# Long convolution's filter in two shifted copies instead of four, loaded early on two queues, and zero products on the score banks

## The chip, the cores and the metric

The kernel runs on one core of a Trainium2 chip. The core has a matrix engine (PE, with its weight loads shown apart as PEld), a vector engine (DVE), a scalar engine that computes activations (ACT), a general engine (POOL), a queue engine that mostly issues DMA transfers (SP), and 16 DMA engines. Each engine works through its own instructions in order and waits on semaphores. The matrix engine writes to PSUM, of eight banks of 128 x 512 float values. The metric is the device time of one execution in microseconds (us), taken over several runs; the profile is one further execution, with its own time.

## What is computed

Two independent parts, whose results stand side by side in the output (2048 x 1024, bf16):

```python
# A: attention over x (2048 x 512), 32 heads of 16
qkv = x @ wqkv
p = softmax(q @ k.T * 16 ** -0.5)          # 32 heads, 2048 x 2048 scores each
a = (p @ v) @ wo
# B: gated long convolution over q, k, v (2048 x 512 each)
k_shift = causal convolution of k with 4 taps (shift_k), per channel
kv = k_shift * v
y  = causal convolution of kv with ssm_k (2048 taps, per channel) + kv * ssm_D
b  = q * y
```

## The kernel before

The program is written out in full by a planner in Python: it walks through *steps* T = 0, 1, 2, ... and keeps a model of the time of each engine (`pe.t`, `act.t`, `dve.t`) to decide which instruction goes into which engine's stream next. On the chip each engine then simply runs its stream in that order. Nothing is decided at run time, so a transfer that lands later than the model thinks makes the engine that needs it wait, and everything behind that instruction in its stream with it. A DMA's landing is modelled as a fixed time after its issue (4 us, `dma`, line 281), and an issue on SP as 0.05 us.

**Attention.** The 2048 score blocks (128 keys x 512 queries of one head, one PSUM bank each) are taken two or three to a step. In step T, PE computes the scores into banks 0 to 2 or 3 to 5 by turns (line 719), ACT takes the exponential of all of them in one instruction (line 726), and two steps later PE multiplies with V into bank 6 or 7 (line 835). One block of some steps is not given to ACT: DVE computes its exponential by bit arithmetic (line 744, then six passes, lines 784 to 791, in sets of two, later four blocks). `dve_choice` (line 646) decides where; before the filter copies are all made (`h_kzall`) it lets DVE be at most 1.0 us behind, after that 8.0 us, and sets of two start at least 4 steps apart until step 90.

**Background work.** In the first half PE also computes the projections K, V and Q from x, in bank 5 until step 55 and bank 7 later; DVE evacuates each such bank (lines 444, 462, 430). PE's next job needs the bank free, and PE works in order: if the evacuation is late, the next scores are late too. From step 128 on PE does the convolution (line 992): for each group of 4 channels and each of 16 lags, four products of 64 columns. When PE would have little to do, `keep_share` (line 1146) adds products of an identity matrix with zeros (line 1160) to a bank where an accumulation is open (bank 6 or 7), since the chip lowers PE's clock when PE idles; `filler_home` says which bank, or none.

**The filter's way.** For the convolution, the 2048 taps of each channel must be there reversed and shifted, as a matrix that PE can read as its moving operand. The taps come in two loads `KZN[0]` and `KZN[1]` (1 MB each; in the profile they appear under the names of the tiles they lie in, QT and EI), and D in one of 1 KB (`DSS`, in the profile JNK); all three raise one semaphore, `h_kzl`. `kz_first` adds D to the first tap on POOL (tile KZ0, in the profile KZ). For each of 4 channel groups c and each of VG = 4 shifts ro, that is for 16 copies i, `kz_turn` writes a reversed copy in runs of VG values into slot i % 4 of `KZS` (tile WR in the profile): two large DVE copies (`half` 0 and 1, line 512) and a small one (line 518). `kz_store` then stores it to DRAM (`kz_scratch`), on SP; a slot is written again only when its store has landed (`h_kzs.get(i - 4)` in the waits). The pieces are due at steps `KZ_AT + 3 * i + j` (line 539), so copy i = 0 at step 11, copy 4 at step 23 and copy 15 at 56. During the convolution the filter is read back in pieces of 256 KB (line 968) as rows of 1024 values, of which each product takes 64 columns as 64 / VG runs of VG values (line 991).

**The queue SP.** Its first transfers, in this order: x rows 0 to 511; four turned (transposing) loads of x rows 512 to 1023 (`load_x(1)`); the rest of the Q and K weights; four turned loads `load_x(2)`; KZN[0], KZN[1], DSS; four turned loads `load_x(3)`; the first 128 channels of k turned (2048 rows); the first half of v; the next 128 channels of k turned. All stores of filter copies come behind these. ACT issues the first Q and K weights, all V weights and the taps `SHK`, and then begins to compute.

## Time and profile before

| | us |
|---|---|
| median of 3 runs (lowest to highest) | 832.82 (829.57 to 833.69) |
| the profiled execution, its own time | 830.77 |
| its span, from first to last instruction | 828.9 |
| granted clock of PE, mean over the span | 0.994 |

How to read it: rows of groups give line, engine, operation, output tile <- input tiles, shape and count, then busy time and the mean duration of one in ns, then the engine's idle time just before them and who ended it. Rows in order of time begin with start and duration in us; in square brackets stands the idle time before and what ended it. In the windows, the granted clock is 1.00 at full speed. Busy times of PE are modelled and overlap.

### The profile page before, as it was taken

To read this page: it belongs to the slowest core of one execution; us is meant where nothing else is said; L and a number is where in the kernel's file an instruction comes from. 1 tells how busy PE (TensorE), PEld (TensorE's weight loads), DVE (VectorE), ACT (ScalarE), POOL (GpSimd) and SP (SyncE) were. 2 spreads that over 40 slices of the span, in tenths; PEclk is the share of its full clock that TensorE was granted. 3 is DMA by queue.
4 is the path that set the end of the run, shared out by engine and by line. 5 is a ranking of instruction groups with operands and counts; after the bars stand their busy time and mean duration, and the time that the engine had idled before them with its cause. 6 is when DMAs were issued, how large, how long until landed. Compare 5 with 4: busy or idle time off the path is not lost.

```text
span 828.9 us, 29863 instructions
## 1 busy us (share of the span) xinstructions
PE 719.2 (87%) x13409; PEld 320.7 (39%) x13445; DVE 787.6 (95%) x1228; ACT 810.6 (98%) x702; POOL 17.3 (2%) x35
## 2 busy tenths in 40 slices
...
GB/s 244 288 253 269 178 1 48 30 98 282 235 95 195 219 184 216 138 259 296 233 210 274 234 260 263 231 254 238 226 264 307 274 286 299 229 225 187 26 1 26
DMA packets 123855, 167.30 MB, mean 202 GB/s; under 512 B 50384, under 2 KB 55504, under 8 KB 123472
## 3 DMA queue, kind: packets, MB, share of 16 engines
q1 hardware_dynamic: 120752, 162.77, 63.5%
q8 instruction: 106, 1.74, 0.8%
q10 hardware_dynamic: 2400, 1.05, 0.5%
...
## 4 chain that ended last, share of the span: by engine, by line
ACT 88%; DVE 6%; PE 3%; SPq 2%; DMA 1%; issue 0%; POOL 0%; DVEq 0%
ACT PT L726 88%; DVE WR L512 2%; SPq L286 2%; DMA JNK<-in_B_ssm_D_dram 1%; PE PS L719 1%; PE PS L835 1%; DVE EI L744 1%; DVE KTo L444 0%; DVE KV L487 0%; DVE EA L787 0%; DVE WR L518 0%; DVE VAF L462 0%; PE PS L916 0%; DVE EA L784 0%; DVE EI L791 0%
## 5 line engine op out<-in xcount | busy, mean ns | idle before, releaser
L726 ACT ACTIVATE PT<-PS 128x1536 bf16<-128x1536 f32 (+1 forms) x695 | 806.5, 1432 | 7.3 <-PE PS L719 6.8
L719 PE MATMUL PS<-QT,KTo 32*128 32x512 bf16 x2048 | 273.0, 386 | 91.0 <-ACT PT L726 67.6
L835 PE MATMUL PS<-PT,VAF 128*32 128x512 bf16 x1782 | 227.8, 391 | 1.0 <-DVE STG L883 0.4
L992 PE MATMUL PS<-WR,KV 128*8 128x64 bf16 (+15 forms) x8192 | 182.7, 213 | 0.2
L992 PEld LDWEIGHTS PS<-WR,KV 128*18 128x18 bf16 (+15 forms) x8192 | 150.1, 119 | 43.9 <-issue 22.5
L719 PEld LDWEIGHTS PS<-QT,KTo 32*128 32x128 bf16 x2048 | 69.3, 91 | 243.2 <-ACT PT L726 224.0
L744 DVE TENSOR_SCALAR EI<-PS 128x512 int32<-128x512 f32 x206 | 136.6, 684 | 1.9 <-PE PS L719 1.2
L791 DVE SCALAR_TENSOR_TENSOR EI<-EI,EA 128x1024 int32<-128x1024 int32 (+1 forms) x90 | 92.1, 1040 | 0.0
L835 PEld LDWEIGHTS PS<-PT,VAF 128*32 128x32 bf16 x1782 | 53.4, 93 | 90.0 <-issue 84.0
L1160 PE MATMUL PS<-ZR,IDN 128*128 128x512 bf16 (+3 forms) x290 | 79.6, 329 | 0.2 <-issue 0.2
L790 DVE TENSOR_TENSOR EA<-EA,xT 128x1024 bf16<-128x1024 f16 (+1 forms) x53 | 46.7, 895 | 0.0
L835 PE MATMUL PS<-EI,VAF 128*32 128x512 bf16 x206 | 45.1, 411 | 1.8 <-DVE VAF L462 1.2
L787 DVE TENSOR_TENSOR EA<-EA,xT 128x1024 f16<-128x1024 f16 (+1 forms) x53 | 46.6, 896 | 0.0
L744 DVE TENSOR_SCALAR xT<-PS 128x512 int32<-128x512 f32 x60 | 39.9, 686 | 0.5 <-PE PS L719 0.2
L784 DVE TENSOR_SCALAR xT<-EI 128x1024 f16<-128x1024 uint16 (+1 forms) x46 | 37.8, 849 | 0.4
L1160 PEld LDWEIGHTS PS<-ZR,IDN 128*128 128x128 bf16 x290 | 22.7, 97 | 30.5 <-issue 20.4
L791 DVE SCALAR_TENSOR_TENSOR EI<-EI,WKV 128x1024 int32<-128x1024 int32 x28 | 34.1, 1219 | 0.0
L788 DVE TENSOR_SCALAR xT<-xT 128x1024 f16<-128x1024 f16 (+1 forms) x53 | 27.0, 527 | 0.0
L786 DVE TENSOR_SCALAR EA<-xT 128x1024 f16<-128x1024 f16 (+1 forms) x53 | 26.7, 527 | 0.0
L790 DVE TENSOR_TENSOR WKV<-WKV,STG 128x2048 bf16<-128x2048 f16 x21 | 25.5, 1215 | 0.0
L787 DVE TENSOR_TENSOR WKV<-WKV,STG 128x2048 f16<-128x2048 f16 x21 | 25.5, 1212 | 0.0
L883 DVE STREAM_TRANSPOSE STG<-PS 128x512 f32<-128x512 f32 x31 | 22.0, 711 | 2.8 <-PE PS L835 2.6
...
## 6 DMA issues: line engine op xcount, KB each, us to landing
WR<-kz_scratch SPq DMA_DIRECT2D x512, 256.0 KB, 4.1
kz_scratch<-WR SPq DMA_DIRECT2D x16, 752.0 KB, 4.2
...
QT<-in_B_ssm_k_dram SPq DMA_DIRECT2D x1, 1024.0 KB, 5.6
EI<-in_B_ssm_k_dram SPq DMA_DIRECT2D x1, 1024.0 KB, 8.8
STG<-in_B_v_dram SPq DMA_DIRECT2D x1, 1024.0 KB, 7.3
```

What stands on the lines that cost most here:

```text
L719: ins = e.matmul(PS[:, bank, :], lhsT=KTo[32 * s:32 * s + 32, g // 2, kt * 128:(kt + 1) * 128], rhs=QT[32 * s:32 * s + 32, qb % 2, g, :], ...
L726: h_exp[T] = act.op(lambda e: e.activation(PT[:, T % R_PT, 0:n * QB], PS[:, banks[0]:banks[0] + n, :].rearrange("p b f -> p (b f)"), ACT.E ...
L744: s.fix.append(dve.op(lambda e: e.tensor_scalar(ei_of(i)[:, 0, :], PS[:, bank, :], FIX_LO, FIX_ADD, ALU.max, ALU.add), [h] + old + [x for ...
L784: step(2, lambda sl: lambda e: e.tensor_scalar(eb[:, sl], frac[:, sl], FS / OCT, -FS * ROOT0, ALU.mult, ALU.add), s.fix + old)
L786: step(4, lambda sl: lambda e: e.tensor_scalar(ea[:, sl], eb[:, sl], FS * (ROOT0 - ROOT1), None, ALU.add))
L787: step(2, lambda sl: lambda e: e.tensor_tensor(ea[:, sl], ea[:, sl], eb[:, sl], ALU.mult))
L788: step(4, lambda sl: lambda e: e.tensor_scalar(eb[:, sl], eb[:, sl], C1 * BITS / FS ** 3, (C0 + C1 * ROOT0) * BITS / FS ** 2, ALU.mult, AL ...
L790: step(2, lambda sl: lambda e: e.tensor_tensor(eg[:, sl], ea[:, sl], eb[:, sl], ALU.mult))
L791: step(1, lambda sl: lambda e: e.scalar_tensor_tensor(ei[:, sl], ei[:, sl], BITS / OCT, eg[:, sl], ALU.mult, ALU.add), ends=True)
L835: ins = e.matmul(PS[32 * s:32 * s + 32, pvb(qb * NG + g), :], lhsT=VAF[:, kt, h * VW:h * VW + 32], rhs=rhs, start=(order[b] == 0), stop=(o ...
L992: ins = e.matmul(PS[32 * c:32 * c + NW - 2 * n, BGB, col:col + 64], lhsT=KV[:, 2 * n:NW, 4 * qd + c], rhs=w, start=(n == 0), stop=(n == NB ...
L1160: return e.matmul(PS[:, bank, col:col + 128 * k], lhsT=IDN[:, :], rhs=ZR[:, :].rearrange("p (m d) -> p m d", m=1).broadcast_to([128, 4 * k ...
```

## The change

- `VG` becomes 2: for each channel group two shifted copies instead of four, so 8 copies of 95 x 16 x 2 = 3040 values (760 KB) instead of 16 of 47 x 16 x 4 = 3008 (752 KB). The large DVE copies write (and read, reversed) runs of 2 values, of 1440 and 1410 elements; the convolution's products read 32 runs of 2 in place of 16 runs of 4.
- The loads: DSS and KZN[0] are issued by ACT behind `SHK`; KZN[1] by SP ahead of `load_x(2)`; each KZN has its own semaphore. The rest of the Q and K weights moves behind `load_x(2)`. The model takes the loads to land at `KZ_LANDS`.
- The pieces are due from step `KZ_AT` = 4: copy i at step 4 + 3 i, so copy 4 at step 16 and the last, copy 7, at 25, and only once the model's DVE has come to the landing of the load. `kz_first` is done for each load by itself. The second half of v, the last channels of k, the read-back and the load of q follow the last copies, as before, and so come earlier.
- The products that make kv for the first two channel groups are due some steps later.
- `keep_share`: where `filler_home` gives no bank, the new `zeros_on_scores` adds zero products to the first score bank of the step, as long as by the model they end 0.14 us before that step's exponential starts; the exponential waits for them, too. This holds from step 56 on.
- `LAG_US`, the model's time for one lag of four products, goes from 0.068 to 0.075.

```diff
@@ -26,7 +26,7 @@
 C = 512
 NB = S // 128
 NW = 2 * NB
-VG = 4
+VG = 2
 NGR = (128 - VG) // VG + 64 // VG
 LKZ = NGR * NB * VG
 LROW = 64 * NB
@@ -78,7 +78,7 @@
 FIX_BEHIND = 1.6
 NEXT = -0.1
 PV_HOLD = 3
-LAG_US = 0.068
+LAG_US = 0.075
 SPAN = 3.4
 SHARE = 0.9
 SLACK = 0.06
@@ -98,9 +98,11 @@
 SET_US = 0.72
 PART_US = 0.6
 KZ_US = .57
-KZ_AT = 11
+KZ_AT = 4
+KZ_LANDS = 11.5, 14.5
 KZ_OVER = 0.0
 FINISH = 8
+ZERO_GAP = .14
 TURN_BLKS = 9
 TURN_AFTER = 4
 STALL = 0.3
@@ -301,7 +303,8 @@
     d_x = [DmaSem(sem(f"d_x{i}")) for i in range(4)]
     d_kt = [DmaSem(sem(f"d_kt{i}")) for i in range(4)]
     d_v = [DmaSem(sem(f"d_v{i}")) for i in range(2)]
-    d_tap, d_kz, d_wo = [DmaSem(sem(n)) for n in ("d_tap", "d_kz", "d_wo")]
+    d_tap, d_wo = [DmaSem(sem(n)) for n in ("d_tap", "d_wo")]
+    d_kz = [DmaSem(sem(f"d_kz{i}")) for i in range(2)]
     d_kzw = [DmaSem(sem(f"d_kzw{i}")) for i in range(4)]
     d_q = [DmaSem(sem(f"d_q{i}")) for i in range(C // CH)]
     d_outB = [DmaSem(sem(f"d_outB{i}")) for i in range(C // CH)]
@@ -328,13 +331,14 @@
     load_x(1)
     h_wv = dma(act, d_w[2], WV, wview[:, :, 2 * D:3 * D])
     h_shk = dma(act, d_tap, SHK[:, :, :], B_shift_k.rearrange("(c p) m -> p c m", p=128))
+    kzview = B_ssm_k.rearrange("(p c) s -> p c s", c=4)
+    dma(act, d_kz[0], DSS, B_ssm_D.rearrange("(p c m) -> p c m", c=4, m=1))
+    h_kzl = []
+    for i, q in enumerate((act, sp)):
+        h_kzl.append(dma(q, d_kz[i], KZN[i], kzview[:, 2 * i:2 * i + 2, :], us=KZ_LANDS[i] - q.t))
+    load_x(2)
     h_wq.append(dma(sp, d_w[3], WQ[:, :, 128:D], wview[:, :, 128:D]))
     h_wk.append(dma(sp, d_w[4], WK[:, :, 128:D], wview[:, :, D + 128:2 * D]))
-    load_x(2)
-    kzview = B_ssm_k.rearrange("(p c) s -> p c s", c=4)
-    for i in range(2):
-        dma(sp, d_kz, KZN[i], kzview[:, 2 * i:2 * i + 2, :])
-    h_kzl = dma(sp, d_kz, DSS, B_ssm_D.rearrange("(p c m) -> p c m", c=4, m=1))
     load_x(3)
     h_kt = {0: turn_in(d_kt[0], KTR[0][:, 16:LKT], k2[:, 0:128])}
     h_v2 = {0: dma(sp, d_v[0], VLO, v2[0:1024, :].rearrange("(t p) d -> p t d", p=128))}
@@ -495,48 +499,48 @@
 
     h_kzw = [None]
 
-    h_kzt, h_kzs = [None], {}
-
-    def kz_first():
-        for i in range(2):
-            h = pool.op(lambda e, i=i: e.tensor_copy(KZ0[:, 2 * i:2 * i + 2, 64:192], KZN[i][:, :, 0:128]), [h_kzl])
-        h_kzt[0] = pool.op(lambda e: e.tensor_tensor(KZ0[:, :, 64:65], KZ0[:, :, 64:65], DSS, ALU.add), [h])
+    h_kzt, h_kzs = {}, {}
+
+    def kz_first(i):
+        cc = slice(2 * i, 2 * i + 2)
+        h = pool.op(lambda e: e.tensor_copy(KZ0[:, cc, 64:192], KZN[i][:, :, 0:128]), [h_kzl[i], h_kzl[0]])
+        h_kzt[i] = pool.op(lambda e: e.tensor_tensor(KZ0[:, cc, 64:65], KZ0[:, cc, 64:65], DSS[:, cc, :], ALU.add), [h])
 
     def kz_turn(i, half):
         c, ro = i // VG, i % VG
-        g0, g1 = (0, 24) if half == 0 else (24, NGR)
+        g0, g1 = (0, (NGR + 1) // 2) if half == 0 else ((NGR + 1) // 2, NGR)
         o = 255 - ro - VG * g0
         k = KZN[c // 2][:, c % 2, o:o + 1]
         k = bass.AP(tensor=k.tensor, offset=k.offset, ap=[k.ap[0], [-VG, g1 - g0], [128, NB - 1], [-1, VG]])
-        hs = [h_kzl, h_kzs.get(i - 4)]
+        hs = [h_kzl[c // 2], h_kzs.get(i - 4)]
         h = dve.op(lambda e: e.tensor_copy(KZS[:, i % 4, g0:g1, 1:NB, :], k), hs, us=KZ_US)
         if half == 0:
             return
         o = 191 - ro
         k0 = KZ0[:, c, o:o + 1]
         k0 = bass.AP(tensor=k0.tensor, offset=k0.offset, ap=[k0.ap[0], [-VG, NGR], [-1, VG]])
-        h_kzp[i] = dve.op(lambda e: e.tensor_copy(KZS[:, i % 4, :, 0, :], k0), [h_kzt[0], h_kz0] + hs, us=0.19)
+        h_kzp[i] = dve.op(lambda e: e.tensor_copy(KZS[:, i % 4, :, 0, :], k0), [h_kzt[c // 2], h_kz0] + hs, us=0.19)
         kz_store(i)
-        if i == 7:
+        if i == 2 * VG - 1:
             load_vhi()
 
     def kz_store(i):
         c, ro = i // VG, i % VG
         h_kzs[i] = dma(sp, d_kzw[i % 4], kz_ap[:, ro, :].rearrange("(p c) m -> p c m", c=4)[:, c, :],
                        KZS[:, i % 4, :, :, :].rearrange("p g n v -> p (g n v)"), [h_kzp[i]])
-        if i == 15:
+        if i == 4 * VG - 1:
             h_kzall[0] = True
             for c in range(2, 4):
-                h_kt[c] = turn_in(d_kt[c], KTR[c][:, 16:LKT], k2[:, 128 * c:128 * c + 128], [h_kzs[12], h_kzs[13]])
-                h_kt0[1] = pool.op(lambda e, c=c: e.memset(KTR[c][:, 0:16], 0.0), [h_kzs[12], h_kzs[13]])
+                h_kt[c] = turn_in(d_kt[c], KTR[c][:, 16:LKT], k2[:, 128 * c:128 * c + 128], [h_kzs[4 * VG - 4], h_kzs[4 * VG - 3]])
+                h_kt0[1] = pool.op(lambda e, c=c: e.memset(KTR[c][:, 0:16], 0.0), [h_kzs[4 * VG - 4], h_kzs[4 * VG - 3]])
 
     h_kzp, h_kzall = {}, [False]
 
     def load_vhi():
-        h_v2[1] = dma(sp, d_v[1], VHI, v2[1024:S, :].rearrange("(t p) d -> p t d", p=128), [h_kzp[7]])
-
-    kv_pieces = [(8, kz_first)]
-    kz_pieces = [(KZ_AT + 3 * i + j, KZ_US + 0.22 * j, lambda i=i, j=j: kz_turn(i, j)) for i in range(16) for j in range(2)]
+        h_v2[1] = dma(sp, d_v[1], VHI, v2[1024:S, :].rearrange("(t p) d -> p t d", p=128), [h_kzp[2 * VG - 1]])
+
+    kv_pieces = [(KZ_AT - 2, lambda: kz_first(0)), (KZ_AT, lambda: kz_first(1))]
+    kz_pieces = [(KZ_AT + 3 * i + j, KZ_US + 0.22 * j, lambda i=i, j=j: kz_turn(i, j), i // 4) for i in range(4 * VG) for j in range(2)]
     kv_pieces.sort(key=lambda x: x[0])
 
 
@@ -695,7 +699,7 @@
             chunk_of[b] = (T, j)
         chunks.append((bl, banks_of[T]))
 
-    h_exp = {}
+    h_exp, exp_at, fills = {}, {}, {}
     h_blk = {}
     h_ptfree, pt_used = {}, {}
 
@@ -719,7 +723,7 @@
                 ins = e.matmul(PS[:, bank, :],
                                lhsT=KTo[32 * s:32 * s + 32, g // 2, kt * 128:(kt + 1) * 128],
                                rhs=QT[32 * s:32 * s + 32, qb % 2, g, :],
-                               start=True, stop=True, tile_position=(32 * s, 0))
+                               start=True, stop=bank != banks[0] or not fills.get(T), tile_position=(32 * s, 0))
             return ins
         h = pe.op(fn, deps, us=0.32)
         n = len(bl) - (bl[-1] in on_dve)
@@ -727,6 +731,7 @@
                                                  PS[:, banks[0]:banks[0] + n, :].rearrange("p b f -> p (b f)"),
                                                  ACT.Exp, scale=math.log(2.0) / OCT),
                           [h] + h_ptfree.get(T - R_PT, []), us=0.41 * n + 0.1)
+        exp_at[T] = act.t - (0.41 * n + 0.1)
         assert T < R_PT or pt_used[T - R_PT] == sum(b not in on_dve for b in chunks[T - R_PT][0])
         for b, bank in zip(bl[:n], banks):
             bank_free[bank] = h_blk[b] = h_exp[T]
@@ -738,7 +743,7 @@
     def exp_on_dve(b, bank, h, T):
         s, i = on_dve[b]
         assert s.free()
-        old = [h_kzp[15]] if s.off < 4 and not any(o.off < 4 for o in sets if o is not s) else []
+        old = [h_kzp[4 * VG - 1]] if s.off < 4 and not any(o.off < 4 for o in sets if o is not s) else []
         if s.off >= 8 and not s.over:
             old = [st0["x12"]]
         s.fix.append(dve.op(lambda e: e.tensor_scalar(ei_of(i)[:, 0, :], PS[:, bank, :], FIX_LO, FIX_ADD, ALU.max, ALU.add),
@@ -965,7 +970,7 @@
             qd, c, r, h = wr_parts.pop(0)
             src = bass.AP(tensor=kz_ap.tensor, offset=kz_ap[4 * qd + c, 0, 0].offset,
                           ap=[[NB * VG, 128 // VG], [LKZ, VG], [1, LROW]])
-            h_wr[qd] = dma(sp, d_wr[r], WR[r][:, c, :], src, [h_kzs[i] for i in range(12, 16)] + [h] + hold, takes=SET_US)
+            h_wr[qd] = dma(sp, d_wr[r], WR[r][:, c, :], src, [h_kzs[i] for i in range(4 * VG - 4, 4 * VG)] + [h] + hold, takes=SET_US)
             if c == 3:
                 land[qd] = when_of(h_wr[qd])
 
@@ -1095,7 +1100,7 @@
     n_unit = 4 // UNIT
     todo += [(when(0, 2 * o, 4 * sc) - 4, x_at[sc], n_unit, unit_job("k", o, sc)) for o in range(4) for sc in range(4) if o or sc]
     todo += [(when(0, 2 * o, 0) - 4, 0, n_unit, unit_job("q", 0, o)) for o in range(1, 4)]
-    todo += [(((58, 61, 64, 67), (88, 100, 106, 112), (94, 118, 124, 146), (100, 134, 140, 152))[c][j], max(18 + 2 * c if c < 2 else 64, 40 if j >= 2 else 0), 2, prod_job(c, j))
+    todo += [(((64, 66, 70, 74), (96, 108, 118, 126), (94, 118, 124, 146), (100, 134, 140, 152))[c][j], max(18 + 2 * c if c < 2 else 64, 40 if j >= 2 else 0), 2, prod_job(c, j))
              for c in range(4) for j in range(4)]
     todo += [(when(qb, 2 * o, 0) - 2 - EARLY if qb != 2 else X2_AT + 8 * o, max(when(qb - 2, 2 * o + 1, 15, 3) + 6 if qb > 1 else 140 + 16 * (o // 2), 0),
               n_unit, unit_job("q", qb, o)) for qb in range(1, NQB) for o in range(4)]
@@ -1145,7 +1150,10 @@
 
     def keep_share(T, lim):
         home = filler_home(T)
-        if home is None or T >= NT:
+        if T >= NT:
+            return
+        if home is None:
+            zeros_on_scores(T, lim)
             return
         bank, col, start, dep = home
         busy = sum(u for t, u in pe.last if t > lim - SPAN)
@@ -1161,6 +1169,26 @@
                                 rhs=ZR[:, :].rearrange("p (m d) -> p m d", m=1).broadcast_to([128, 4 * k, 32]),
                                 start=start, stop=start)
             pe.op(fn, [h_zr, h_idn, dep], us=0.02 + 0.0565 * k)
+
+    def zeros_on_scores(T, lim):
+        if T < N_EARLY:
+            return
+        bank = chunks[T][1][0]
+        while True:
+            us = 0.02 + 0.0565 * 4
+            busy = sum(u for t, u in pe.last if t > lim - SPAN)
+            if pe.t + us > min(lim, exp_at[T] - ZERO_GAP) or busy > SHARE * SPAN:
+                return
+            fills.setdefault(T, []).append(len(fills.get(T, [])))
+            i = len(fills[T]) - 1
+
+            def fn(e, i=i):
+                return e.matmul(PS[:, bank, :], lhsT=IDN[:, :],
+                                rhs=ZR[:, :].rearrange("p (m d) -> p m d", m=1).broadcast_to([128, 16, 32]),
+                                start=False, stop=i == len(fills[T]) - 1)
+            h = pe.op(fn, [h_zr, h_idn], us=us)
+            act.ops[-1][0].append(h)
+            act.seen[id(h[0])] = h[1]
 
     def emit_bg(T, lim):
         bg_step(T, lim)
@@ -1183,7 +1211,7 @@
         if h_kzall[0]:
             load_wr(T)
             if not h_qn:
-                load_qn(0, [h_kzp[15]])
+                load_qn(0, [h_kzp[4 * VG - 1]])
         st["time"] = min(st["time"] + (0.78 if T >= CONV_AT else 0.4 if T >= N_EARLY else 0.45), 1.1)
         rest = NB * C // 4 - NB * st["qd"] - st["lag"]
         if T >= N_EARLY:
@@ -1348,7 +1376,7 @@
             dve_fill.pop(0)[1]()
         while kv_pieces and T >= kv_pieces[0][0]:
             kv_pieces.pop(0)[1]()
-        while kz_pieces and T >= kz_pieces[0][0] and (dve.t + kz_pieces[0][1] <= end + KZ_OVER or T >= kz_pieces[0][0] + 4):
+        while kz_pieces and T >= kz_pieces[0][0] and dve.t >= when_of(h_kzl[kz_pieces[0][3]]) - 0.1 and (dve.t + kz_pieces[0][1] <= end + KZ_OVER or T >= kz_pieces[0][0] + 4):
             kz_pieces.pop(0)[2]()
     assert (st["qd"], st["turn"], st["op"]) == (C // 4, C // 32, len(later_op)) and not later and not todo, (st, todo)
     assert not dve_later and not kv_pieces and not dve_fill and not end_ops
```

## The prediction, made before the changed kernel was run

> **What bounds the kernel.** I read the page first: busy times, the chain that ended last, the costliest groups.
>
> ```profile
> span 828.9 us, 29863 instructions
> PE 719.2 (87%) x13409; PEld 320.7 (39%) x13445; DVE 787.6 (95%) x1228; ACT 810.6 (98%) x702; POOL 17.3 (2%) x35
> ...
> ACT 88%; DVE 6%; PE 3%; SPq 2%; DMA 1%; issue 0%; POOL 0%; DVEq 0%
> ...
> L719 PE MATMUL PS<-QT,KTo 32*128 32x512 bf16 x2048 | 273.0, 386 | 91.0 <-ACT PT L726 67.6
> ...
> L992 PE MATMUL PS<-WR,KV 128*8 128x64 bf16 (+15 forms) x8192 | 182.7, 213 | 0.2
> ...
> L1160 PE MATMUL PS<-ZR,IDN 128*128 128x512 bf16 (+3 forms) x290 | 79.6, 329 | 0.2 <-issue 0.2
> ```
>
> ACT computes exponentials for 98% of the span, and 88% of the chain is ACT. PE waits 67.6 us for ACT and fills 79.6 us more with products by zero. DVE (95%) takes the exponentials of those score banks that it has time for. So only two things shorten the kernel: fewer banks on ACT, or fewer gaps between ACT's instructions. The second view is ACT alone in order of time (each row starts behind a gap, in brackets), with the sum of its waits, and the groups by shape:
>
> ```profile
> 8.80 17.27 ACT L726 ACTIVATE PT<-PS 128x1536 bf16<-128x1536 f32 x15 [0.74 <-PE PS L719]
> 27.52 1.02 ACT L726 ACTIVATE PT<-PS 128x1024 bf16<-128x1024 f32 x1 [1.45 <-PE PS L719]
> 29.60 1.94 ACT L726 ACTIVATE PT<-PS 128x1024 bf16<-128x1024 f32 x2 [1.05 <-PE PS L719]
> 32.03 12.08 ACT L726 ACTIVATE PT<-PS 128x1024 bf16<-128x1024 f32 x11 [0.50 <-PE PS L719]
> ...
> 74.61 7.31 ACT L726 ACTIVATE PT<-PS 128x1536 bf16<-128x1536 f32 x6 [0.88 <-PE PS L719]
> ...
> 703.83 118.03 ACT L726 ACTIVATE PT<-PS 128x1024 bf16<-128x1024 f32 x102 [1.38 <-PE PS L719]
> ```
> ```profile
> ACT PT L726 <- PE PS L719: 6.8, 9, 1.4
> ```
> ```profile
> L726 ACT ACTIVATE PT<-PS 128x1536 bf16<-128x1536 f32 x392 | 552.4, 1612 | 2.2 <-PE PS L719 1.9
> L726 ACT ACTIVATE PT<-PS 128x1024 bf16<-128x1024 f32 x303 | 308.4, 1198 | 5.1 <-PE PS L719 4.9
> ```
>
> All gaps together are 6.8 us: 1.45 + 1.05 + 0.50 = 3.0 between 26 and 32 us, 0.88 at 74, 1.38 at 702, 0.74 at the start, and the rest, 0.8, is small ones. A bank moved from ACT to DVE saves 1612 - 1198 = 0.41 us. These are all the prizes there are, some tenths of a per cent each. The third view is what made the 3.0 us: the order of time around 24 us, and windows of 1 us.
>
> ```profile
> 23.91 1.18 DVE L512 COPY WR<-QT 128x1440 bf16<-128x1440 bf16 x2 [2.84 <-DMA JNK<-in_B_ssm_D_dram]
> ...
> 25.65 0.25 DVE L518 COPY WR<-KZ 128x188 bf16<-128x188 bf16 x1 [0.56 <-POOL KZ L503]
> ...
> 25.82 0.68 DVE L462 CAST VAF<-PS 128x512 bf16<-128x512 f32 x1
> ...
> 26.78 0.38 PE L408 MATMUL PS<-xT,WKV 128*128 128x512 bf16 x1 [2.51 <-DVE VAF L462]
> ```
> ```profile
> 10.00:20.00 10.00, 8.77 (x69) 3.30 (x68) 2.35 (x5) 10.00 (x11) 4.03 (x4) 1.00 0.99 293
> ```
> ```profile
> 28.00:29.00 1.00, 1.00 (x9) 0.16 (x7) 0.00 (x0) 0.54 (x1) 0.00 (x0) 0.50 0.90 286
> ...
> 702.00:703.00 1.00, 1.00 (x21) 0.40 (x16) 0.44 (x1) 0.45 (x1) 0.00 (x0) 0.50 0.92 285
> ```
>
> (Columns: stretch, its length, busy time of PE, PE's weight loads, DVE, ACT and POOL, granted clock, share of the DMA engines, GB/s.)
>
> DVE arrives at the first filter copy (step 11) at 21.07 and waits 2.84 us for the filter's loads. The evacuation of a V bank stands behind it and starts 4.75 us after the wait began; PE, in order, waits for the bank; ACT runs dry 1.45 us, and because PE was idle its granted clock is 0.50, which makes the next two gaps. The same clock stands beside the gap of 702.
>
> **The change, part by part.** First, the old wait goes. The two filter loads are issued behind ACT's early issues and at 6.5 us on SP, in place of 14.1 and 14.7, behind less traffic: -3.0 us. ACT's queue issues two more loads ahead of its first work, 0.6 us each (the rows of SP below); some of it falls into ACT's wait for the first transposes, so I take +0.2, bounds 0 and 1.2. The first copy now comes at step 4: with 17.27/15 = 1.15 us a step that is 13.4 us. The load took 8.8 us from issue (row below), so it may land at 13 to 15.5: +0.5, bounds 0 and 1.5.
>
> Second, and I think decisive, **the wait that takes its place**. The copies use four slots, and copy 4 must wait until the store of copy 0 has landed. Copy 4 moves from step 23 to step 16, that is to 8.80 + 16 x 1.15 - 0.4 = 26.8 us (the 0.4 as step 11: 21.07 against 21.45). The store is issued by SP behind all loads:
>
> ```profile
> 1.26 5.15 SPq L286 DMA_TRANSPOSE xT<-in_A_x_dram  x4
> 6.46 0.58 SPq L286 DMA_DIRECT2D WQ<-in_A_wqkv_dram  x1
> 7.08 1.43 SPq L286 DMA_DIRECT2D WKV<-in_A_wqkv_dram  x1
> ...
> 14.11 0.58 SPq L286 DMA_DIRECT2D QT<-in_B_ssm_k_dram  x1
> ...
> 15.69 7.72 SPq L286 DMA_TRANSPOSE xT<-in_A_x_dram  x4
> 23.45 2.05 SPq L286 DMA_TRANSPOSE WR<-in_B_k_dram  x1
> ...
> 26.18 6.51 SPq L286 DMA_TRANSPOSE WR<-in_B_k_dram  x1
> 32.73 19.96 SPq L286 DMA_DIRECT2D kz_scratch<-WR  x8
> ```
> ```profile
> 80.20 5.98 SPq L286 DMA_TRANSPOSE WR<-in_B_k_dram  x2
> ```
> ```profile
> kz_scratch<-WR SPq DMA_DIRECT2D x16, 752.0 KB, 4.2
> ...
> EI<-in_B_ssm_k_dram SPq DMA_DIRECT2D x1, 1024.0 KB, 8.8
> ```
>
> Copy 0 was complete at 25.9, yet its store was issued at 32.73: SP was still issuing turned loads. The change takes one filter load and the D load from SP: of the three issues between 14.11 and 15.69 one stays, so 1.05 us go, and 31.7 is the late end. The early end lets every turned load go at its quickest, 5.15 for four of x and 5.98/2 for the second of k, and 0.6 for a plain load as at 6.46: 6.46 + 0.6 + 5.2 + 2.1 + 5.2 + 2.1 + 0.6 + 3.0 = 25.3. With 4.2 us to land, the store is there between 29.5 and 35.9, always after 26.8. The bytes ahead of it are the same, so I take a point nearer the late end: issued 29.3, landed 33.5. DVE then stands from 26.8 to 33.5, and with half a copy (0.5) evacuations come 7.2 us late. Before, 4.75 us of lateness gave a first gap of 1.45, so 3.3 us are covered by what PE and ACT still have; 7.2 - 3.3 = 3.9, and 1.55 for the clock as before: +5.5 us, bounds 0 (at 29.5) and 7.8 (at 35.9). Copies 5 to 7 come 3 steps apart, stores 2 to 3 us apart, so I price no wait there. Behind copy 4 on DVE stand all evacuations of K and V and the first exponentials.
>
> Third, DVE's work. Rows: all L512 copies, their slowest kind, L518, and the kinds that make up one exponential on DVE.
>
> ```profile
> sum 829.00, DVE 20.33; mean DVE 1.20
> ```
> ```profile
> L512 DVE COPY WR<-EI x2: 715/716/716, 62.9 to 63.5; 128x1440 bf16<-128x1440 bf16 x1, 128x1380 bf16<-128x1380 bf16 x1
> ```
> ```profile
> L518 DVE COPY WR<-KZ x16: 236/243/251, 25.6 to 79.5; 128x188 bf16<-128x188 bf16 x16
> ```
> ```profile
> L791 DVE SCALAR_TENSOR_TENSOR EI<-EI,EA 128x512 int32<-128x512 int32 x6 | 4.1, 689 | 0.0
> ...
> L744 DVE TENSOR_SCALAR EI<-PS 128x512 int32<-128x512 f32 x6 | 4.0, 673 | 0.0
> ...
> L790 DVE TENSOR_TENSOR EA<-EA 128x512 bf16<-128x512 f16 x6 | 2.5, 422 | 0.0
> ...
> L788 DVE TENSOR_SCALAR EA<-EA 128x512 f16<-128x512 f16 x6 | 1.6, 291 | 0.0
> ```
>
> Now 20.3 + 16 x 0.24 = 24.2 us. Afterwards 16 half copies of as many elements and 8 small ones. No row has runs of two; the nearest is the slowest, 0.716, where a run straddles words: 16 x 0.716 + 8 x 0.24 = 13.4, so 10.8 us are freed. Bounds: 0.53 us a copy, the quickest (14 us freed), and one element at a time as in L744, 1440/512 x 0.673 = 1.9 us, where DVE loses 8. An exponential takes 673 + 689 + 3 x 422 + 2 x 291 = 3.2 us (three passes as L790, two as L788), so 10.8 us are 3.4 banks, 1.4 us of ACT. Also four copies move to before 27 us, where DVE was mostly idle (2.35 of 10 us between 10 and 20): I take -1.6, bounds +1.0 and -2.5. With DVE freer between 36 and 80 the gap at 74 and the small ones shrink: -0.9 of 1.7, bounds 0 and -1.7.
>
> Fourth, zeros on score banks. They give PE work where its other home for zeros is closed, as before 702: -1.5 (1.38 and what the clock left behind), bounds -1.5 and, for exponentials that wait for zeros, +5 (rival below). Fifth, the filter product reads runs of two. No row shows it; the planner's constant goes from 0.068 to 0.075, which on 182.7 us would be +18; from below 0, from above twice, +183. It lies beside PE's 67.6 + 79.6 = 147 us of waiting and zeros, so I take 0 on the path. The products moved to later due steps (64 to 126) stay ahead of step 128, where the convolution starts; 0.
>
> **Sum** on the profiled execution, 830.8 us (span 828.9 and 1.9 around it), which lies 2.0 below the median of the runs: -3.0 + 0.2 + 0.5 + 5.5 - 1.6 - 0.9 - 1.5 = -0.8. On the median, 832.8 - 0.8 = **832.0**.
>
> **Rivals.** *The new wait is short*, because SP is through its loads near 25.3 us: 5.5 becomes 0 to 1, and the time 827. For it: the two filter loads no longer fill the queue in front of x3, which took 7.72 us for what once took 5.15. Against it: the second turned k took 6.51 us where an idle queue takes 3.0, with the same loads ahead of it.
>
> *The new wait is long* (slower): the store is late as now, lands at 36.5 or later, DVE stands 9.7 us, the gap is 9.7 + 0.5 - 3.3 + 1.55 = 8.5 in place of 5.5, and with one more 1.2 for the next copy, whose store is as late, 832.0 + 3.0 + 1.2 = 836.2. It outweighs all gains from a landing at 34.3 on. For it: the same bytes lie ahead of the store. Against it: of the 32.7 us some, as the 7.72 at x3, were waits in a queue that is filled otherwise now. [...]
>
> *PE becomes the bound*: if a lag of the filter product costs over 80% more (147 of 182.7), the rest is on the path; twice gives 183 - 147 = +36, 869. For it only that DVE's copies slow from 0.53 to 0.72 with the start of a run. [...]
>
> *Zeros delay exponentials*: each now waits for the last zero on its bank. If PE is 0.15 us behind its plan in 60 steps, 60 x 0.15 = +9, 841.
>
> *It does not do what it says*: the filter loads, amid the other early traffic, land no earlier than DVE's new first copy by 5 us or more, and the old wait only moves: 833.
>
> **Chances.** As forecast 0.45 (own range 828 to 836), short wait 0.27, long wait 0.14, PE 0.04, zeros 0.06, nothing moved 0.04. Over 0.5% (4.2 us, about what can be told from no change) faster: most of the short wait and a sixth of the forecast, 0.31; slower: a part of the long wait, PE, most of the zeros, the forecast's upper end, 0.20; within, 0.49. The range runs from 823 (short wait 826.5, no first wait and nothing at the start -0.7, best copies -0.9, no small gaps -0.8, and 1 for the spread of runs) to 841 (zeros late).
>
> **What would show it.** Right: no wait for the D load near 21 us; a DVE wait for the store kz_scratch<-WR from about 27 to 33 us, an ACT gap of 3 us or more after it and clock 0.50; the first store issued at 28 to 31; copies of 0.53 to 0.72 us; some three banks more on DVE; no gap of 1.4 near 702. Wrong: no such wait, L992 well over 200 us, or ACT gaps all over the middle of the span.

## The result and the profile after

| | before | after |
|---|---|---|
| median of 6 runs each, us (lowest to highest) | 831.5 (829.57 to 833.69) | 841.02 (839.38 to 842.73) |
| ratio, 95% interval | | 1.0118 (1.0100 to 1.0136) |
| the profiled execution, its own time, us | 830.77 | 841.44 |
| its span, us | 828.9 | 839.6 |
| granted clock of PE, mean | 0.994 | 0.990 |

The kernel became 1.2% slower, where the forecast was no change. The page of the changed kernel, in the rows that stand in the prediction for the kernel before (the lines of code shown have moved by 2 to 5):

```profile
span 839.6 us, 29786 instructions
## 1 busy us (share of the span) xinstructions
PE 747.7 (89%) x13364; PEld 335.7 (40%) x13400; DVE 792.6 (94%) x1235; ACT 810.7 (97%) x702; POOL 17.9 (2%) x36
...
ACT 80%; DVE 8%; PE 4%; SPq 4%; DMA 2%; issue 1%; DVEq 0%; ACTq 0%
...
L997 PE MATMUL PS<-WR,KV 128*26 128x64 bf16 (+15 forms) x8192 | 215.1, 240 | 5.2 <-issue 3.3
```

ACT is as busy as before (810.7 against 810.6 us) but has 8 points less of the chain: it stands more. The filter product has become 32 us longer on PE (215.1 against 182.7). ACT in order of time, its exponentials with the gap ahead of each row:

```profile
8.92 8.23 ACT L730 ACTIVATE PT<-PS 128x1536 bf16<-128x1536 f32 x7 [0.75 <-PE PS L723]
18.06 1.02 ACT L730 ACTIVATE PT<-PS 128x1024 bf16<-128x1024 f32 x1 [0.92 <-PE PS L723]
...
23.27 3.86 ACT L730 ACTIVATE PT<-PS 128x1536 bf16<-128x1536 f32 x3 [1.20 <-PE PS L723]
...
41.73 1.45 ACT L730 ACTIVATE PT<-PS 128x1536 bf16<-128x1536 f32 x1 [5.95 <-PE PS L723]
44.63 8.72 ACT L730 ACTIVATE PT<-PS 128x1024 bf16<-128x1024 f32 x8 [1.46 <-PE PS L723]
...
682.99 29.00 ACT L730 ACTIVATE PT<-PS 128x1536 bf16<-128x1536 f32 x25 [0.20 <-PE PS L1186]
712.40 42.73 ACT L730 ACTIVATE PT<-PS 128x1024 bf16<-128x1024 f32 x36 [0.41 <-PE PS L723]
756.01 10.49 ACT L730 ACTIVATE PT<-PS 128x1024 bf16<-128x1024 f32 x9 [0.87 <-PE PS L723]
```

Two clusters of gaps are new: 4.2 us in six gaps from 17 to 32 us, then 5.95 and 1.46. The gap of 1.4 near 702 us is gone. What stands ahead of the clusters, on DVE in order of time, and on SP's queue:

```profile
15.46 1.20 DVE L516 COPY WR<-QT 128x1440 bf16<-128x1440 bf16 x1 [2.31 <-DMA QT<-in_B_ssm_k_dram]
...
38.73 1.44 DVE L516 COPY WR<-EI 128x1440 bf16<-128x1440 bf16 x2 [5.77 <-DMA kz_scratch<-WR]
```
```profile
6.60 0.58 SPq L288 DMA_DIRECT2D EI<-in_B_ssm_k_dram  x1
7.22 10.70 SPq L288 DMA_TRANSPOSE xT<-in_A_x_dram  x4
...
19.14 5.76 SPq L288 DMA_TRANSPOSE xT<-in_A_x_dram  x4
24.94 1.93 SPq L288 DMA_TRANSPOSE WR<-in_B_k_dram  x1
...
27.54 7.27 SPq L288 DMA_TRANSPOSE WR<-in_B_k_dram  x1
34.85 3.44 SPq L288 DMA_DIRECT2D kz_scratch<-WR  x4
```

DVE waits 2.31 us for the first filter load and 5.77 us, from 32.96 on, until the store of copy 0 has landed. That store is issued at 34.85, later than before (32.73), although copy 0 was complete near 18 us: the four turned loads of x behind the filter load take 10.70 us to issue. The same four, which before stood ahead of the filter loads, took 5.51 us there:

```profile
8.56 5.51 SPq L286 DMA_TRANSPOSE xT<-in_A_x_dram  x4
```

This is no accident of one execution. In the eleven profiled executions with a filter load ahead of these four (the changed kernel and the experiments on it) they took 8.4 to 12.0 us, in the nine with the filter loads behind them 5.2 to 5.8. And they follow the filter loads: 8.4 to 8.9 us in the three executions where those landed 8.6 to 9.8 us after issue, 10.7 to 12.0 in the eight where those needed 11.0 to 13.0. What holds the issue up is not shown beyond that.

The filter loads themselves need longer from issue to landing than the 8.8 us of before (issues, with KB and median us to landing):

```profile
kz_scratch<-WR SPq DMA_DIRECT2D x8, 760.0 KB, 6.2
...
QT<-in_B_ssm_k_dram ACTq DMA_DIRECT2D x1, 1024.0 KB, 11.2
EI<-in_B_ssm_k_dram SPq DMA_DIRECT2D x1, 1024.0 KB, 11.6
```

Behind each wait PE stands (1.97 and 6.32 us), and then its clock is at 0.50 for a while. PE in order of time, then windows of 1 us (columns as in the prediction; the clock is the third number from the end):

```profile
17.63 0.39 PE L723 MATMUL PS<-QT,KTo 32*128 32x512 bf16 x2 [1.97 <-DVE VAF L466]
...
41.07 0.61 PE L723 MATMUL PS<-QT,KTo 32*128 32x512 bf16 x3 [6.32 <-DVE EI L749]
```
```profile
17.00:18.00 1.00, 0.37 (x5) 0.24 (x6) 1.00 (x3) 0.14 (x1) 0.20 (x1) 1.00 0.87 256
...
19.00:20.00 1.00, 1.00 (x5) 0.21 (x4) 0.00 (x0) 0.37 (x2) 0.40 (x2) 0.50 1.19 164
27.00:28.00 1.00, 1.00 (x6) 0.24 (x5) 0.00 (x0) 0.23 (x2) 0.00 (x0) 0.50 1.08 175
...
29.00:30.00 1.00, 0.31 (x4) 0.11 (x2) 1.00 (x2) 0.79 (x1) 0.00 (x0) 1.00 0.65 182
```

PE stood 1.97 us, and from 19 to 28 us its granted clock was 0.50.

**An account that can be made of every run.** ACT computes exponentials from its first to the end of its last, and 7.0 to 7.6 us follow. So the span is the start of the first exponential, plus ACT's gaps, plus the exponentials, plus that end. From the rows of ACT in order of time, in us (gaps before and after 90 us; "exponentials" holds the gaps that are too short for a row). Each row is one profiled execution; executions of one kernel lie up to 11 us apart (before: 827.3 to 838.4), so a difference of 1 or 2 us between two rows is a hint and not a result.

| kernel, all as profiled | first starts | gaps to 90 | gaps after 90 | exponentials | span |
|---|---|---|---|---|---|
| before | 8.8 | 4.7 | 1.4 | 807.0 | 828.9 |
| after | 8.9 | 13.9 | 2.1 | 807.7 | 839.6 |
| both waits out, steps 8 and 27 (e9) | 9.0 | 3.6 | 1.0 | 807.0 | 827.7 |
| store wait out, load wait left (e7) | 9.0 | 7.3 | 2.5 | 807.6 | 833.5 |
| load wait out, store wait left (e8) | 9.5 | 13.4 | 3.8 | 806.7 | 840.5 |
| both waits out, first copy at step 15 (e1) | 9.7 | 4.1 | 0.4 | 806.1 | 827.5 |
| e9, copies further apart (e11) | 9.1 | 3.7 | 3.1 | 807.1 | 830.1 |
| e9, copies planned as 0.80 us (e18) | 9.4 | 2.7 | 2.6 | 806.4 | 828.2 |
| after, no zeros on score banks (e3) | 9.1 | 14.4 | 3.8 | 807.6 | 842.0 |
| e9, no zeros (e10) | 9.3 | 4.5 | 3.8 | 807.3 | 832.0 |
| before, zeros alone (e12) | 9.0 | 3.7 | 0.0 | 806.7 | 826.5 |
| before, runs of two alone (e4) | 8.8 | 7.4 | 1.1 | 806.4 | 830.8 |
| before, first copy at step 15 (e13) | 9.0 | 5.1 | 4.7 | 809.5 | 835.4 |
| e13, late products later (e14) | 9.1 | 1.8 | 5.6 | 808.8 | 832.4 |
| e14 with zeros (e15) | 9.3 | 1.8 | 2.3 | 808.8 | 829.8 |
| e4, first copy at step 15 (e16) | 9.1 | 4.1 | 2.9 | 807.1 | 830.8 |
| e16 with zeros (e17) | 9.0 | 4.1 | 0.6 | 806.6 | 827.4 |
| e17, copies planned as 0.87 us (e19) | 9.1 | 1.4 | 0.4 | 809.1 | 827.1 |

The changed kernel's 10.7 us over before are 9.2 in the gaps to 90 us, 0.7 in later gaps and 0.7 in the exponentials.

### The profile page after: what moved, and what is told of

It is laid out like the page before. It is cut to its first block, busy times and chain, and to the rows that moved or that the text cites. A ratio compares the mean times of both kernels' runs of the same rounds, so it can differ in the third digit from the quotient of the medians.

```text
span 839.6 us, 29786 instructions
## 1 busy us (share of the span) xinstructions
PE 747.7 (89%) x13364; PEld 335.7 (40%) x13400; DVE 792.6 (94%) x1235; ACT 810.7 (97%) x702; POOL 17.9 (2%) x36
## 4 chain that ended last, share of the span: by engine, by line
ACT 80%; DVE 8%; PE 4%; SPq 4%; DMA 2%; issue 1%; DVEq 0%; ACTq 0%
ACT PT L730 80%; SPq L288 4%; PE PS L723 1%; PE PS L997 1%; DMA WR<-kz_scratch 1%; DVE EI L749 1%; PE PS L840 1%; DVE EI L796 1%; DVE WR L516 1%; DMA kz_scratch<-WR 0%; DVE xT L749 0%; DVE EA L792 0%; DVE WKV L792 0%; DVE xT L789 0%; DVE EA L795 0%
## 5 line engine op out<-in xcount | busy, mean ns | idle before, releaser
L730 ACT ACTIVATE PT<-PS 128x1536 bf16<-128x1536 f32 (+1 forms) x695 | 806.8, 1393 | 17.6 <-PE PS L723 16.5
L723 PE MATMUL PS<-QT,KTo 32*128 32x512 bf16 x2048 | 273.3, 387 | 70.2 <-ACT PT L730 38.7
L997 PE MATMUL PS<-WR,KV 128*26 128x64 bf16 (+15 forms) x8192 | 215.1, 240 | 5.2 <-issue 3.3
L997 PEld LDWEIGHTS PS<-WR,KV 128*22 128x22 bf16 (+15 forms) x8192 | 166.4, 119 | 47.4 <-issue 24.8
L749 DVE TENSOR_SCALAR EI<-PS 128x512 int32<-128x512 f32 x214 | 142.4, 683 | 3.1 <-PE PS L723 2.4
L796 DVE SCALAR_TENSOR_TENSOR EI<-EI,EA 128x1024 int32<-128x1024 int32 (+1 forms) x98 | 96.9, 1009 | 0.0
L1168 PE MATMUL PS<-ZR,IDN 128*128 128x512 bf16 (+3 forms) x242 | 68.0, 336 | 0.2 <-DVE STG L881 0.2
L840 PE MATMUL PS<-EI,VAF 128*32 128x512 bf16 x214 | 47.4, 406 | 0.2
L749 DVE TENSOR_SCALAR xT<-PS 128x512 int32<-128x512 f32 x56 | 37.2, 681 | 1.0 <-PE PS L723 0.6
L1168 PEld LDWEIGHTS PS<-ZR,IDN 128*128 128x128 bf16 x242 | 18.7, 97 | 31.4 <-issue 21.5
## 6 DMA issues: line engine op xcount, KB each, us to landing
QT<-in_B_ssm_k_dram ACTq DMA_DIRECT2D x1, 1024.0 KB, 11.2
EI<-in_B_ssm_k_dram SPq DMA_DIRECT2D x1, 1024.0 KB, 11.6
```

Of the source, the lines that this page charges most:

```text
L723: ins = e.matmul(PS[:, bank, :], lhsT=KTo[32 * s:32 * s + 32, g // 2, kt * 128:(kt + 1) * 128], rhs=QT[32 * s:32 * s + 32, qb % 2, g, :], ...
L730: h_exp[T] = act.op(lambda e: e.activation(PT[:, T % R_PT, 0:n * QB], PS[:, banks[0]:banks[0] + n, :].rearrange("p b f -> p (b f)"), ACT.E ...
L749: s.fix.append(dve.op(lambda e: e.tensor_scalar(ei_of(i)[:, 0, :], PS[:, bank, :], FIX_LO, FIX_ADD, ALU.max, ALU.add), [h] + old + [x for ...
L796: step(1, lambda sl: lambda e: e.scalar_tensor_tensor(ei[:, sl], ei[:, sl], BITS / OCT, eg[:, sl], ALU.mult, ALU.add), ends=True)
L840: ins = e.matmul(PS[32 * s:32 * s + 32, pvb(qb * NG + g), :], lhsT=VAF[:, kt, h * VW:h * VW + 32], rhs=rhs, start=(order[b] == 0), stop=(o ...
L997: ins = e.matmul(PS[32 * c:32 * c + NW - 2 * n, BGB, col:col + 64], lhsT=KV[:, 2 * n:NW, 4 * qd + c], rhs=w, start=(n == 0), stop=(n == NB ...
```

## The experiments

Times are medians; each ratio is to the kernel before on the same chip, with its 95% interval. The experiments ran on several chips, on which the medians of the kernel before were 830.3 to 831.7 us, so between runs on different chips the ratios are the better comparison.

**Both waits out.** In the changed kernel the first copy goes to step 15; all else stays (e1).

```diff
-KZ_AT = 4
+KZ_AT = 15
```

> The changed kernel with the filter copies due from step 15 on in place of 4, all else as it is. Two-waits theory (the first copy waits 2.3 us for its load, copy 4 5.8 us for the store of copy 0, and each leaves PE at half clock): both waits vanish, ACT's gaps before 50 us shrink from 11.6 us to under 1.5 us, and the time falls from 841 to 829-832. Rival (the product that reads runs of two, 215 us of PE in place of 183, and what it makes late): the gaps before 50 us matter little, 838 or more.

Measured: 831.16 us, 0.9990 (0.9971 to 1.0009). DVE waits for no DMA. So without the waits the loss is gone; what else the change does on PE costs nothing that can be seen, with the filter product at 220 us. But nothing is gained either, and the rest of the study is about that as much as about the waits.

**One wait at a time.** Copies 4 to 7 later (e7), copies 0 to 3 a little later (e8), both (e9).

```diff
-    kz_pieces = [(KZ_AT + 3 * i + j, ...
+    kz_pieces = [(KZ_AT + 3 * i + (11 if i >= 4 else 0) + j, ...        # e7
+    kz_pieces = [(KZ_AT + 3 * i + (3 - i if i < 4 else 0) + j, ...      # e8
+    kz_pieces = [(KZ_AT + 4 + 3 * i + (7 if i >= 4 else 0) + j, ...     # e9
```

> The changed kernel with copies 4 to 7 taken at the steps 27, 30, 33 and 36 in place of 16, 19, 22 and 25; copies 0 to 3 as changed. If the two waits of VectorE, 2.3 us for the load and 5.8 us for the store, each cost the ScalarE gaps that follow them (4.2 and 7.4 us), then only the second goes: no wait for the store, ScalarE's gaps before 35 us stay near 4.2 us, and the time is 841.0 - 7.4 = about 833.5 us (832.5 to 835). If the first wait alone started the whole loss (the clock at half speed from 18.8 us on, and all that is late behind it), the time stays above 837.

Measured: 832.53 us, 1.0010 (0.9985 to 1.0035). Behind the load wait, the store wait is worth 841.0 - 832.5 = 8.5 us.

> The changed kernel with copies 0 to 3 taken at the steps 7, 9, 11 and 13 in place of 4, 7, 10 and 13; copies 4 to 7 as changed, so that copy 4 still waits for the store of copy 0. If the two waits add, the 4.2 us behind the first go and the 7.4 us behind the second stay: about 837 us (835.5 to 838). If the second wait is there only because the first makes SP's queue late, both go and the time is 830 to 833. If the first is worth what was predicted for it, 0.5 us, the time stays at 840.5.

Measured: 842.99 us, 1.0141 (1.0101 to 1.0181), four executions from 839.6 to 846.4, which fits none of the three. The load wait is gone and nothing is won. DVE in order of time, SP's queue, and windows of 10 us of this kernel:

```profile
36.19 1.44 DVE L516 COPY WR<-EI 128x1440 bf16<-128x1440 bf16 x2 [7.45 <-DMA kz_scratch<-WR]
```
```profile
32.29 3.43 SPq L288 DMA_DIRECT2D kz_scratch<-WR  x4
```
```profile
30.00:40.00 10.00, 2.16 (x14) 0.69 (x14) 3.81 (x7) 2.37 (x3) 0.00 (x0) 0.73 1.09 381
40.00:50.00 10.00, 9.67 (x46) 3.07 (x44) 7.97 (x20) 6.39 (x6) 0.00 (x0) 0.50 1.00 342
```

The kernel now arrives at copy 4 at 28.7 in place of 33.0 us, and waits 7.45 us in place of 5.77 for a store that SP still issues only at 32.3. The end of the second wait is set by SP's queue; the first wait only took up time that would have been waited there. The waits do not add.

> The changed kernel with copies 0 to 3 at the steps 8, 11, 14 and 17 and copies 4 to 7 at 27, 30, 33 and 36: neither wait is met, and the copies are spread as thin as can be over VectorE's early work. If the two waits are all that the early order loses, the time is that of the version that begins at step 15 (831.2) or less, down to 829 if the smaller bunching frees ScalarE's small gaps; if the stores in among the loads cost something of themselves, it is 833 or more.

Measured: 830.39 us, 0.9991 (0.9974 to 1.0008). With e7, e8 and the changed kernel this makes all four cases:

| | no store wait | store wait |
|---|---|---|
| no load wait | 830.4 (e9) | 843.0 (e8) |
| load wait | 832.5 (e7) | 841.0 (after) |

The load wait alone is worth 2.1 us (the intervals of e7 and e9 overlap) and beside the store wait nothing. The store wait alone is worth 12.6 us, behind the load wait 8.5. Both together are worth 10.6.

**The stores past SP's queue.** The first four stores issued by POOL (e2).

```diff
-        h_kzs[i] = dma(sp, d_kzw[i % 4], kz_ap...
+        h_kzs[i] = dma(pool if i < 4 else sp, d_kzp[i] if i < 4 else d_kzw[i % 4], kz_ap...
```

> The changed kernel with the stores of copies 0 to 3 issued by POOL in place of SP. If copy 4 waits because the store stands in SP's queue behind loads that are still being issued: the stores go at 19 to 31 us, the wait of 5.8 us falls below 1.5 us, the gap of 5.95 and the one after it go, 833-835. If it waits for the bytes ahead of it at the 16 DMA engines: the wait stays over 3 us, 838 or more.

Measured: 834.1 us, 1.0030 (1.0003 to 1.0057), the runs far apart (831.1 to 840.6). The profiled execution is the slowest of them, so it shows where it goes wrong when it does. POOL, SP, DVE and PE in order of time:

```profile
17.88 0.71 POOL L288 DMA_DIRECT2D kz_scratch<-WR  x1
```
```profile
24.34 13.65 SPq L288 DMA_TRANSPOSE WR<-in_B_k_dram  x1
```
```profile
34.87 0.95 DVE L517 COPY WR<-EI 128x1440 bf16<-128x1440 bf16 x1 [3.35 <-DMA kz_scratch<-WR]
```
```profile
40.57 1.06 PE L413 MATMUL PS<-xT,WKV 128*128 128x512 bf16 x2 [6.84 <-DVE EA L796]
```

The first store goes out at 17.88 in place of 34.85, copy 4 waits for nothing, and 7 us are won on the median. But other transfers became longer: stores now take 14.4 us to land (6.2 in the changed kernel), the first turned load of k takes 13.65 us to issue (1.93 there), copy 5 waits 3.35 us, and a K projection of PE waits 6.84 us. DVE is named there, though it was at work on other things; the tile xT is what that product reads, and the turned loads of x that fill it land 7.9 us after issue in the median (5.9 in the changed kernel). Which transfer ended this wait is not shown. The issue of the first store came 17 us earlier, since SP's queue was held up until then; what holds the other transfers up is not shown either.

**The zeros on score banks**, taken from the changed kernel (e3), from e9 (e10), and added alone to the kernel before (e12).

```diff
         if home is None:
-            zeros_on_scores(T, lim)
             return
```

> The changed kernel without zero products on score banks. The trace shows three of them in the whole span, so: within 1 us of the changed kernel, 840-842, and no new drop of the clock. If these three keep the clock up at important places, or if waiting for them costs: over 2 us of difference to either side.

Measured: 844.57 us, 1.0164 (1.0144 to 1.0185): 3.5 us more, where the changed kernel has just three such products in its span (0.39 us each, from 185 to 683 us).

> The changed kernel with both waits taken out by later copies (steps 8 to 17 and 27 to 36), and without the three zero products on score banks. If those three are worth of themselves what their absence cost beside the waits, 3.5 us, the time is 834 us. If the prediction's 1.5 us for the one gap near 702 us holds, 832. If their absence cost only because other clock drops were there already, the time stays at 830.4.

Measured: 831.33 us, 1.0004 (0.9979 to 1.0029), 0.9 over e9.

> The kernel before with nothing but the zero products on score banks. If they fill the stretch ahead of 702 us and so save the gap of 1.4 us there, the time is 830 us, 1.4 below the kernel before, and the clock in 700 to 710 us is above 0.9. If the gap has another cause, the time stays within 0.5 us of the kernel before.

Measured: 829.12 us, 0.9977 (0.9957 to 0.9997). ACT of this kernel has no gap behind 82 us that the view shows:

```profile
73.81 7.31 ACT L727 ACTIVATE PT<-PS 128x1536 bf16<-128x1536 f32 x6 [0.88 <-PE PS L720]
81.38 738.03 ACT L727 ACTIVATE PT<-PS 128x1536 bf16<-128x1536 f32 x633 [0.26 <-PE PS L720]
```

In all pairs, those further down included, the zeros shorten the gaps after 90 us (1.4 to 0.0, 3.8 to 1.0, 3.8 to 2.1, 5.6 to 2.3, 2.9 to 0.6), and the medians by 0.9 to 3.5 us; only e12 against before, and the changed kernel against e3, have recorded intervals that stand apart.

**Where the gain of the removed load wait went.** Runs of two alone on the kernel before (e4); the early loads alone (e5); the kernel before with its copies after the load (e13), and with the products of the last two channel groups kept from coming before step 72 (e14), and zeros too (e15); runs of two with late copies and without early loads (e16), and with zeros (e17).

```diff
-VG = 4
+VG = 2            # e4, e16, e17; 4 again in e5
-KZ_AT = 11
+KZ_AT = 15        # e13 to e17
-max(18 + 2 * c if c < 2 else 64, ...
+max(18 + 2 * c if c < 2 else 72, ...        # e14, e15
```

> The kernel before with two shifted copies in runs of two, and nothing else of the change (loads, due steps, constants as before). Two-waits theory: the old gaps of 3.0 us stay, DVE gains some 9 us and 3 banks, 829-832, though L992 takes 215 us. Rival (runs of two on PE): 835 or more, with gaps or slower steps from 180 us on.

Measured: 831.97 us, 1.0018 (1.0000 to 1.0035). No gain from half the copies, and by the account 2.7 us more of gaps before 90 us.

> The changed kernel with four copies and runs of four values again (16 copies of a quarter each), the first at step 11 as before, no zeros on score banks, and the modelled delay and due steps of before: what is left of the change is that the filter is loaded among the first, on two queues. No DVE wait for the filter load near 21 us. If that wait of 3 us set 3 us of the time, as the prediction has it, the time is 829 us; if the gap only moves to the next shortage (the loads of x that now land later, a wait for a store), it stays within 831 to 833.

Measured: 830.4 us over ten executions (827.1 to 833.6), 0.9988 (0.9962 to 1.0014). The eleventh, the profiled one, took 840.3 us; it stands apart and only its queue SP is used above.

> The kernel before with the first copy at step 15 in place of 11: its load has landed by then (first wait 2.84 us at 23.9 us), and nothing else is changed. If that wait is worth the 3 us of the prediction's first term, the time is 828.5 us. If VectorE's time behind it is what counts, and the copies only make up for the gap elsewhere, the time stays within 1 us of the kernel before.

Measured: 837.47 us, 1.0084 (1.0054 to 1.0114). The load wait is gone, but what was won by 85 us, 2.9 us, is lost again in one place. ACT of e13, then PE:

```profile
41.92 14.36 ACT L726 ACTIVATE PT<-PS 128x1024 bf16<-128x1024 f32 x13 [0.71 <-PE PS L719]
...
89.50 2.79 ACT L726 ACTIVATE PT<-PS 128x1536 bf16<-128x1536 f32 x2 [3.38 <-PE PS L719]
```
```profile
87.88 1.03 PE L475 MATMUL PS<-OUTA,WR 128*128 128x128 bf16 x8 [3.25 <-DMA WR<-in_B_k_dram]
```

The last two quarters of k are loaded, turned, into the slots of the filter copies and behind the last store. With every copy four steps later they land later, and the product that reads them stands at 87.88. The rest of e13's loss is 3.3 us more of gaps after 90 us and exponentials longer by 2.5.

> The kernel before with the first copy at step 15 in place of 11, and with the products of the last two quarters of channels allowed from step 72 in place of 64, since with the copies moved TensorE stood 3.3 us at 87.9 us for their turned filter rows. If the load wait near 24 us is worth the 3 us of the prediction's first term once nothing else is made late, the time is 828 us. If the gain is given back wherever VectorE is full, it is that of the kernel before within 1 us.

Measured: 832.94 us, 1.0025 (1.0003 to 1.0046). Now the early gaps are 1.8 in place of 4.7 us: there are the 3 us. But the later gaps are 5.6 in place of 1.4, spread from 179 to 753 us, and the exponentials 1.8 longer. DVE takes 264 banks here in place of 266, which is 0.8 of the 1.8 us; what makes the later gaps stays open.

> The same with the zero products on score banks: 1.2 us less than without them, as on the kernel before; about 827 us if the load wait gives its 3 us, 829 if not.

Measured: 831.49 us, 0.9999 (0.9977 to 1.0021).

> Two copies with runs of two in the kernel before, the filter loaded where it was (behind x's second 512 rows), first copy at step 15, no zeros on score banks: the changed kernel without its early loads and without waits. If the early loads give back what the removed wait saves, by bringing x later, this is faster than the version with early loads and no zeros (831.3 against before 830.3): about 828. If VectorE is full from 30 us on and that decides, it stays at 830 to 831.

Measured: 832.04 us, 1.0017 (0.9999 to 1.0034). So it isn't the early loads that take the gain: without them it is as with them (e10, 831.33).

> The same with the zero products on score banks: 1.2 us less; if it is under 828 us it beats both kernels.

Measured: 829.94 us, 0.9996 (0.9976 to 1.0017).

With runs of two, the gaps to 90 us are 2.3 to 2.7 us longer than with runs of four (e4 against before, e16 against e14; and e13, which differs from e16 in nothing but the runs, has 1.8 us of them up to 85 us), whether a load wait stands there or not. These gaps belong to the plan and are no scatter: the first six behind 32 us agree within 0.02 us in the profiles of e1, e16 and e17, whose copies are planned alike. Two causes were tried on them: that the copies are too close together (e11), and that the planner takes them for shorter than they are (e18 on e9, e19 on e17).

```diff
+    kz_pieces = [((8, 11, 14, 17, 27, 31, 35, 39)[i] + (1 if i < 4 else 2) * j, ...        # e11
-KZ_US = .57
+KZ_US = .80       # e18
+KZ_US = .87       # e19
```

> The changed kernel with copies 0 to 3 at the steps 8, 11, 14 and 17 and copies 4 to 7 at 27, 31, 35 and 39, their two halves two steps apart, so that VectorE has fewer copies between 40 and 62 us, where ScalarE's small gaps stood with the closer order (3.5 us of them). If those gaps come from copies bunched where VectorE is already full, half of them go and the time is 828.5 to 829.5. If VectorE is full there whatever the order, the time stays at 830.4.

Measured: 831.96 us, 1.0011 (0.9990 to 1.0032), early gaps 3.7 us as in e9. It is not the spacing.

> The changed kernel with both waits taken out (copies at 8 to 17 and 27 to 36), and with the planner's duration of a half copy at 0.80 us in place of 0.57; measured are 0.87. If ScalarE's 3.6 us of gaps before 90 us come from a plan that takes the longer copies for shorter than they are, 1.5 us or more of them go and the time is 828.5 to 829. If not, the gaps and the time stay (830.4).

Measured: 831.72 us, 1.0008 (0.9989 to 1.0026). Early gaps fell from 3.6 to 2.7 us, by 0.9 where 1.5 or more was expected; later ones rose from 1.0 to 2.6, and the time did not fall.

> Runs of two with the filter loaded where it was, first copy at step 15, zeros on score banks, and the planner's duration of a half copy at 0.87 us. Against 829.9 without the last: 828 to 828.5 if the plan's short copies are the cause of the 4.1 us of gaps before 90 us, 829.9 if not.

Measured: 829.11 us, 0.9972 (0.9952 to 0.9992): 0.8 us below e17 on the medians, which come from different chips, and 2.0 by the ratios, whose intervals overlap. The gaps before 90 us fell from 4.1 to 1.4 us, so in this kernel they hang on the planned duration. But in the profiled execution the exponentials became 2.5 us longer. Groups on DVE, e17 and then e19 (the first step of an exponential on DVE; one for each bank):

```profile
L746 DVE TENSOR_SCALAR EI<-PS 128x512 int32<-128x512 f32 x212 | 141.4, 684 | 1.3 <-PE PS L720 0.5
L746 DVE TENSOR_SCALAR xT<-PS 128x512 int32<-128x512 f32 x56 | 37.3, 682 | 0.5 <-PE PS L720 0.2
```
```profile
L746 DVE TENSOR_SCALAR EI<-PS 128x512 int32<-128x512 f32 x206 | 136.8, 681 | 2.5 <-PE PS L720 2.2
L746 DVE TENSOR_SCALAR xT<-PS 128x512 int32<-128x512 f32 x60 | 39.4, 680 | 0.5 <-PE PS L720 0.5
```

A planner that takes the copies as longer gives DVE two banks less, 266 in place of 268: 0.8 of the 2.5 us. What makes the rest is not shown. Both banks are missing in the first 90 us, where DVE takes 12 in place of 14. So the gaps may be gone because the plan is truer there, or because DVE is asked for less; no run parts the two. e19 and e12 are faster than before, by 0.3 and 0.2%, with intervals that just exclude no difference.

## Why the prediction was wrong

It said -0.8 us; measured are +9.5. The 10.3 us between them lie in two steps: 10.6 - 6.0 = 4.6 in the waits, and 6.8 - 1.0 = 5.8 in the gains.

**The failed step: "the wait that takes its place", and with it the load wait ahead of it.** Priced 5.5 and 0.5, together 6.0; measured 10.6 (after against e9). The term that was mis-sized is the issue of the first store. The mechanism was right: copy 4 waits for the store of copy 0, which waits behind SP's turned loads; ACT has a gap of over 3 us, and the clock is at 0.50 behind it. The size was wrong. The store was put at 29.3 us, between 25.3 and 31.7, on the ground that "the bytes ahead of it are the same" and that two issues fewer stand on SP; it came at 34.85, and at 32.3 to 35.8 in the ten profiled executions with the early loads and the store on SP, always past the late end. In the order of before it came at 32.5 to 34.2: taking two loads out of SP's queue won nothing for what stands behind. What was overlooked is how much longer turned loads take to issue behind the filter loads: four took 10.70 us, not 5.2. The 7.72 us of before, behind the same loads, were a sign of it, and were taken for waits in a queue that would be "filled otherwise now". The filter loads, for which 8.8 us were taken from the profile of before, needed 11.2 and 11.6 in the company of the first loads. So the load wait was 2.3 us and cost more than its bounds allowed (2.1 us alone, against 0 to 1.5), though beside the store wait it costs nothing (e8). The store wait costs 8.5 us behind it and 12.6 alone, both over its upper end of 7.8; the two terms were added, and the runs show that they do not add. The rival "the new wait is long", 836.2, is what happened, and it was too small: it let the store land at 36.5, and it landed at 38.7. The late end that the prediction gave the landing, 35.9, was nearer than its 33.5 and still too early.

**The second: gains that were added as if each were ACT's.** Without the waits the sum says -3.0 + 0.2 - 1.6 - 0.9 - 1.5 = -6.8; measured are -1.0 (e9 against 831.42).
- The old wait, -3.0: it goes, as said, and e14 shows its 3 us in the early gaps. But no kernel without it became faster by as much. In that early time DVE is idle (2.35 us of work in the window from 10 to 20 in the prediction); behind it, it has little to spare (95% busy over the span). What takes the gain there is not shown as a whole: in e14 it is 4.2 us of later gaps and 1.8 of exponentials, in the profile of e19 2.7 us of saved gaps stand against 2.5 us of longer exponentials.
- Smaller gaps, -0.9: wrong in sign. Runs of two make 2.3 to 2.7 us more of them, and the plan reckons with half copies of 0.57 us, which took 0.65 in runs of four and now take 0.88. With the duration put near that, the gaps fell by 2.7 us in e19 and by 0.9 in e18, so it is a cause, and not shown to be the only one.
- Zeros, -1.5: right in size. -1.2 alone (e12), and the gap near 702 is gone. In the changed kernel the later gaps are 2.1 us all the same; without zeros they are 3.8, so something else in it raised them.
- DVE's freed time, -1.6: DVE took 270 banks in place of 266, about as said, but the saving was eaten. The copies were taken as 0.716 us by the nearest row, and runs of two are slower than any row of before (groups by shape of the changed kernel):

```profile
L516 DVE COPY WR<-QT 128x1440 bf16<-128x1440 bf16 x4 | 3.9, 966 | 2.3 <-DMA QT<-in_B_ssm_k_dram 2.3
L516 DVE COPY WR<-EI 128x1440 bf16<-128x1440 bf16 x4 | 3.4, 859 | 5.8 <-DMA kz_scratch<-WR 5.8
L516 DVE COPY WR<-EI 128x1410 bf16<-128x1410 bf16 x4 | 3.4, 856 | 0.0
L516 DVE COPY WR<-QT 128x1410 bf16<-128x1410 bf16 x4 | 3.4, 854 | 0.0
L522 DVE COPY WR<-KZ 128x190 bf16<-128x190 bf16 x8 | 2.4, 301 | 0.0
```

These are 16.5 us; the same rows of before sum to 24.8, so 8.3 us are freed, not 10.8. And an exponential behind a gap takes more of ACT's time than one in a row (1.45 us alone at 41.73, 8.23 / 7 = 1.18 in a row), which goes some way to explain that ACT's total rose by 0.7 in spite of the four banks.

**What held.** The start, +0.2: 0.12. The filter product at 0 on the path: it rose by 32 us, more than the +18 named, to 215, so the sign "L992 well over 200 us" came, but e1 and e9 show no cost. No wait for the D load. The rivals of PE as the bound and of exponentials that wait for zeros did not come (0.2 us waited for L1186 in all). Of the bounds, those of the copies' duration and of the filter product held; those of the landing times, drawn from a profile in which the transfers came in another order, did not.
